# Issuing the seven products of a quarter group one by one, in an order written out for each block

## The chip, the cores and the metric

The kernel runs on one core of one Trainium2 chip, in one launch. The metric is device time in microseconds (us): the median of three runs was 294.25 us (293.95 to 294.44). Times are written to two digits after the point where they come from a trace.

## The reference

Causal attention with sparse masks, followed by a two-layer network with the Mish activation:

```python
def _attn_ref(q, k, v):                      # q, k, v: 8 x 8 x 576 x 64
    scores = scale * np.matmul(q, k.transpose(0, 1, 3, 2))
    mask_local = (rel >= 0) & (rel < stride)                  # heads 0 to 3, stride 32
    mask_strided = (rel >= 0) & (pos[None, :] % stride == pos[:, None] % stride)   # heads 4 to 7
    ...
    attn = softmax(np.where(masks, scores, -1e9))
    return np.matmul(attn, v)

def _moe_ref(x, w_in, w_out):                # x: 4608 x 512, w_in: 512 x 2048, w_out: 2048 x 512
    h = x @ w_in
    g = h * np.tanh(np.log1p(np.exp(h)))     # Mish
    return g @ w_out
```

## The kernel before

**Blocks.** The 4608 tokens are cut into nine blocks of 512, t = 0 to 8. In block t the kernel does three things side by side: the input product of block t (class `Mlp1`), the output product of block t - 1 (class `Mlp2`), and the attention of batch t + 1 (class `Attn`), as long as there is one. Attention works by batches of 576 tokens, and the MLP takes its 512 out of a ring `xT` of four batches. Blocks 0 and 1 have plans of their own, which the change leaves alone; blocks 2 to 8 are run by `run(plan, t)`. Block 2 has the plan `MAIN2`, blocks 3 to 6 `MAIN`, blocks 7 and 8 `PLAIN`, in which no attention is left.

**Seven products.** Each big product is cut into two by two blocks and computed with seven products instead of eight (Strassen's scheme in Winograd's form). It needs sums of the inputs, made by VectorE: `xs` (steps x0 to x3, the transposed tokens), `gs` (n, g1, g2, g3, the activations), and once `wis` and `wos` (the weights). x1 reads x0's result and x3 that of x1. gs1 is written twice: g1 gives what product 6 of the output reads, and g3 overwrites it for product 4. n makes gs0 for the next block, and g1 reads gs0 and the second half of the activations.

**The input product.** It goes by quarter groups g = 0 to 3 of the hidden features. A group uses three PSUM banks: E, al and be. In this order, on the left the plan's letter of before:
- `a`: product 5 into E; cast of E to s5; product 1 into al; copy of al to be by ScalarE
- `b`: product 6 added to al; cast of al to s2; product 3 added to E; VectorE adds E and s2 into one half of `hh`; product 2 added to be
- `c`: product 7 added to al; VectorE adds al and s5 into the other half of `hh`
- `d`: product 4 added to al
- `U`, `W`, `H`: ScalarE's Mish of be, of al and of `hh` into `gT`

A product is four matmuls of 256 columns. The casts run on ScalarE in blocks 1 to 6 and on VectorE in blocks 7 and 8 (`self.eng`). In blocks 2 to 6 groups 0 and 2 share one set of three banks, groups 1 and 3 the other, so that i (product 1) of group 2 has to wait for W of group 0. The set of groups 1 and 3 is also that of the output product of the block before; the set of groups 0 and 2 also serves every second score tile. In blocks 7 and 8 group 1 has the two attention banks and the E of groups 0 and 3.

**The output product.** Its seven products have two halves each of eight matmuls; a letter `m` in a plan issues the next half, in the order of products 1, 5, 2, 6, 3, 7, 4. Products 1, 5, 6 and 4 are copied by ScalarE, products 3 and 7 added by VectorE; the result goes out by SyncE's DMA queue.

**Attention.** `q0` to `q2` make the scores of the strided heads, `q3` to `q5` those of the local heads: matmuls into a pair of banks, two exps on ScalarE (tile `Ps` or `Pl`), and the mask's multiplication in place (line 287), from block 3 on by GpSimd. `v` issues the next of 13 steps: five products with V of the strided heads (v1 to v5 in the prediction; VectorE divides each by its row sum, lines 314 and 319), two transposes back, then four and two for the local heads. These steps take the banks A0 and A1 in turn. `s` spreads and shares V in its buffers (VectorE). `D` issues the DMA transposes of the next batch, `R` its loads on GpSimd's queue. `e` and `f` load ScalarE's tables for exp and for Mish.

**What sets the order.** A plan is a string of steps. Each engine gets its instructions in the order in which the steps stand, and works them off in that order; semaphores hold an instruction until its inputs are there and its buffer is free. Nothing reorders them. So a plan's order is the order of each queue.

Of the kernel before, what the change touches and what calls it, by code (L numbers as in the profile page):

```python
# [45 lines left out]
def kernel(ctx, tc, q, k, v, moe_w_in, moe_w_out, out):  # L46
    nc = tc.nc
    B, H, S, D = q.shape
# [6 lines left out]
    PE, Po, Dv, Sc = nc.tensor, nc.gpsimd, nc.vector, nc.scalar  # L55
# [6 lines left out]
    def sb(shape, name, dt=BF16):  # L62
        return const.tile(shape, dt, name=name)
# [8 lines left out]
    s2, s5 = [[sb([128, 512], f"{n}{i}", F32) for i in range(2)] for n in ("s2", "s5")]  # L72
# [36 lines left out]
    A0, A1 = bank("at0"), bank("at1")  # L109
# [6 lines left out]
    def cast(eng, out_, in_):  # L116
        if eng is Sc:
            Sc.copy(out_, in_)  # L118
        else:
            eng.tensor_copy(out_, in_)  # L120

    def add(eng, out_, a, b, op=ALU.add):
        eng.tensor_tensor(out=out_, in0=a, in1=b, op=op)  # L123
# [58 lines left out]
    def spread_v(eng):  # L182
        cast(eng, vs[0:PN, :, :, 0:D], vraw[0:PN])
# [197 lines left out]
    class Mlp1:  # L381
# [18 lines left out]
                    )  # L400

        def step(self, s, g):
            z = (self.t + g + 1) % 2
            be, al, E = [x[:] for x in SETS[z]]
            if self.eng is Dv:
                z = ((self.t + 1) % 2, 2, self.t % 2, (self.t + 1) % 2)[g]
                be, al, E = [x[:] for x in ((A1, A0, SETS[(self.t + 1) % 2][2]) if g == 1 else SETS[z])]
            h = hh[z]
            o = gT[:, 4 * g:4 * g + 4, :]
            two = lambda x: x.rearrange("p (u n) -> p u n", u=2)  # L410
            if s == "a":
                self.prod(5, g, E, True)
                cast(self.eng, s5[z][:], E)
                self.prod(1, g, al, True)
                Sc.copy(be, al)  # L415
            elif s == "b":
                self.prod(6, g, al, False)
                cast(self.eng, s2[z][:], al)
                self.prod(3, g, E, False)
                add(Dv, h[:, 0, :], E, s2[z][:])  # L420
                self.prod(2, g, be, False)
            elif s == "c":
                self.prod(7, g, al, False)
                add(Dv, h[:, 1, :], al, s5[z][:])
            elif s == "d":
                self.prod(4, g, al, False)
            elif s == "H":
                Sc.activation(  # L428
                    o[:, :, 256:512], h[:].rearrange("p i (u n) -> p (i u) n", u=2), AF.Mish
                )  # L430
            elif s == "U":
                Sc.activation(o[:, 0:2, 0:256], two(be), AF.Mish)
            elif s == "W":
                Sc.activation(o[:, 2:4, 0:256], two(al), AF.Mish)  # L434
# [130 lines left out]
    with tc.manual_schedule():  # L565
# [6 lines left out]
        B0, B1 = SETS[0][0], SETS[1][0]  # L572

        def unread(n, to, w=512):
            for _ in range(n):
                mm(to[:, 0:w], wis[:, 0, 0, 0, 0:128], wis[:, 0:2, 0, 0, 0:w // 2], True)
# [35 lines left out]
        def plain(t, fc, ps, ccs=(2, 3, 0, 1), act=True):  # L612
            r = (512 * t) % RT
            for cc in ccs:
                mm(
                    ps[:], w_in[:, cc, fc * 128:fc * 128 + 128], xT[:, cc, r:r + 512],
                    start=(cc == 2), stop=(cc == 1),
                )
            if act and ccs[-1] == 1:
                Sc.activation(gT[:, fc, :], ps[:], AF.Mish)  # L620
# [91 lines left out]
        def run(plan, t):  # L712
            b = t + 1
            m1, m2, nxt = Mlp1(t), Mlp2(t - 1), Mlp2(t)
            at = Attn(b) if b < B else None
            if b == B:
                unread(1, A1)
            ms = m2.steps() if t > 1 else []
            bank = [1, 0] if t == 1 else [0, 1]

            def v_steps():
                def pv(kind, r):
                    at.pv(kind, *r, (A0, A1)[bank[0]])
                    bank[0] = (bank[0] + bank[1]) % 2

                def xt(kind, hf):
                    at.xt(kind, hf, (A0, A1)[bank[0]], Sc if t == 1 and kind == "l" else Dv)
                    bank[0] = (bank[0] + bank[1]) % 2
                P = lambda kd, r: (lambda: pv(kd, r))
                X = lambda kd, hf: (lambda: xt(kd, hf))  # L730
                if t == 1:
                    return (
                        [P("l", r) for r in PV_L[:3]] + [X("l", 0), P("l", PV_L[3]), P("s", PV_S[0]), X("l", 1)]
                        + [P("s", r) for r in PV_S[1:]] + [X("s", 0), X("s", 1)]
                    )
                return (
                    [P("s", r) for r in PV_S] + [X("s", 0), X("s", 1)]
                    + [P("l", r) for r in PV_L[:2]] + [X("l", 0)]
                    + [P("l", r) for r in PV_L[2:]] + [X("l", 1)]
                )  # L740
            vs_ = late + (v_steps() if at else [])
            late.clear()
            JOBS = [("s", 0), ("s", 1), ("s", 2), ("l", 0), ("l", 1), ("l", 2)]
            for w in plan.split():
                c, n = w[0], int(w[1:]) if len(w) > 1 else 0
                if c in "abcdHUW":
                    m1.step(c, n)
                elif c == "p":
                    plain(t, n, deal1[n], act=False)
                elif c == "y":  # L750
                    Sc.activation(gT[:, n, :], deal1[n][:], AF.Mish)
                    if deal1[n] is A0:
                        bank[:] = [0, 1]
                elif c == "w":
                    w_out_sums(n, Dv)
                elif c == "m":
                    ms.pop(0)()
                elif c == "x":
                    x_sum(t, n, Dv)
                elif c == "g":  # L760
                    m2.g_sum(n, Dv)
                elif c == "n":
                    nxt.g_sum(0, Dv, 0, 8)
                elif not at:
                    continue
                elif c == "e":
                    Sc.preload_act_table(AF.Exp)
                elif c == "f":
                    Sc.preload_act_table(AF.Mish)
                elif c == "q":  # L770
                    at.qk(*JOBS[n], PAIRS[n % 2 * (1 + (t + 1) % 2)])
                    at.mask(*JOBS[n], Dv if t == 1 or t == 2 and n in (0, 1, 2, 3) else Po)
                elif c == "v":
                    if vs_:
                        vs_.pop(0)()
                elif c == "s":
                    spread_v(Dv)
                    if t > 1:
                        share_v(b, Dv)
                elif c == "h":  # L780
                    share_v(b, Dv)
                elif b + 1 >= B:
                    continue
                elif c == "t":
                    t_step(2, "l", "kq"[n // 2], n % 2, (C[1], C[2], A0, A1)[n], (Sc, Dv)[n % 2])
                    if n == 3:
                        load_qk(3)
                elif c == "D":
                    transpose_by_dma()
                elif c == "R":  # L790
                    hold(kTs, qTs, *((kTl, qTl) if t > 1 else ()))
                    load_vs(b + 1)
                    load_vl(b + 1)
                    if b + 2 < B:
                        load_qk(b + 2)
            assert not ms
            if t == 1:
                late.extend(vs_)
            else:
                for w in vs_:  # L800
                    w()

        late = []
        MAIN = (
            "x0 m m e m m x1 s x2 g1 g2 q0 q1 m m m m g3 q2 q3 m m q4 q5 m D v m f R a0 v v m m v v b0 a1 x3 c0 v "
            "U0 v b1 d0 U1 W0 c1 v a2 d1 W1 v H0 a3 v v b2 v H1 c2 b3 c3 d2 W2 v H3 d3 n U2 U3 W3 H2"
        )
        SECOND = (
            "t0 p0 q2 p1 t1 t2 t3 w1 p2 q3 w2 p3 q5 q4 p4 h p5 p6 f v y0 D y1 p7 s v p8 R y3 y6 v y2 v p9 v v y5 y4 "
            "p10 p11 y9 p12 y8 y7 y11 v v p13 v y13 p14 y10 p15 y14 n v y12 w3 y15"  # L810
        )
        MAIN2 = (
            "v m m v m e v x0 x1 m x2 g1 q1 q0 g2 m m m m g3 q2 s q3 m m q4 q5 m D f v m v a0 R v m m v v b0 a1 x3 "
            "c0 v v b1 d0 U0 U1 W0 c1 v a2 d1 W1 v H0 a3 v v b2 v c2 H1 b3 c3 d2 W2 v H3 d3 U2 U3 W3 H2 n"
        )
        PLAIN = (
            "m m x0 g1 x1 m m x2 x3 a0 m m g2 m b0 m m m g3 m m c0 U0 a1 H0 m m b1 d0 W0 a2 c1 a3 b2 b3 c3 d1 U2 H1 "
            "W1 U1 c2 d3 W3 U3 d2 H2 W2 H3 n"
        )

        for t in range(1, NBLK):
# [40 lines left out]
```

## Time and profile before

| | us |
|---|---|
| median of three runs | 294.25 |
| the profiled execution | 294.54 |
| its span, first to last instruction | 292.8 |
| TensorE busy (matmul ends are modelled) | 282.4 |
| VectorE, ScalarE, GpSimd busy | 205.7, 204.7, 102.7 |
| block 2, from its first half output product to the next block's | 30.31 |
| blocks 3, 4, 5, 6 | 29.60, 29.59, 29.69, 29.80 |
| blocks 7, 8 | 25.20, 25.19 |

In the profile, PE is TensorE's matmuls, PEld its weight loads, DVE VectorE, ACT ScalarE, POOL GpSimd and SP SyncE. A line of the timeline has the start in us, the length in us, the engine, the source line, the operation, the tiles written and read, shapes, and in brackets idle time of the engine before it and what ended it. Every matmul of the two products has line 129, the sums and adds line 123. Rows of one engine overlap a little, since an engine takes up the next instruction before the last one has drained: the interval from start to start tells the rate, the length tells when a result is there.

### The profile page before, as it was taken

What the parts mean: (1) busy time and instruction counts of PE and PEld (TensorE: products, weight loads), DVE (VectorE), ACT (ScalarE), POOL (GpSimd) and SP (SyncE); (2) the same over time, 40 slices, a digit from 0 to 9 for tenths busy, and PEclk for the clock granted to TensorE, in tenths of its full rate; (3) what the DMA queues carried; (4) which work ended last, traced back from release to release, by engine and by line L of the source; (5) the groups of instructions that cost most, each with busy time, mean ns of one, the idle gap of its engine ahead of it and who ended that gap; (6) DMA issues with size and microseconds to landing.
All of it is one profiled execution on the core that took longest, in us unless ns stands there. A gap on an engine that the chain in (4) does not pass through costs nothing.

```text
span 292.8 us, 7799 instructions
## 1 busy us (share of the span) xinstructions
PE 282.4 (96%) x3256; PEld 223.8 (76%) x3268; DVE 205.7 (70%) x387; ACT 204.7 (70%) x361; POOL 102.7 (35%) x109
## 2 busy tenths in 40 slices
PE   8889999999999999999999999999999999999995
PEld 3564545545788888888888888888898888888884
DVE  2583548587798896688768866886688667757842
ACT  2578793769667789778977898789878526825650
POOL 8754330131614533981399039502920000000000
PEclk9999999999999999999999999999999999999999
DMA  7999999999999999999699989950110003003004
GB/s 136 179 204 202 203 194 185 174 169 150 137 154 181 204 174 70 165 223 166 32 167 215 167 39 147 231 36 2 72 73 2 2 29 118 1 3 143 2 0 143
DMA packets 94415, 35.84 MB, mean 122 GB/s; under 512 B 75804, under 2 KB 90124, under 8 KB 94380
## 3 DMA queue, kind: packets, MB, share of 16 engines
q0 software_dynamic: 61712, 18.71, 70.1%
q1 hardware_dynamic: 31708, 15.73, 24.4%
q10 hardware_dynamic: 960, 0.91, 1.0%
q8 instruction: 25, 0.41, 0.6%
q14 instruction: 10, 0.08, 0.1%
HBM read 37.87 MB, written 9.44 MB: 162 GB/s over the span
## 4 chain that ended last, share of the span: by engine, by line
PE 77%; ACT 8%; DVE 7%; issue 3%; DMA 3%; POOL 1%; ACTq 0%; POOLq 0%
PE al L129 34%; PE ee L129 19%; PE be L129 12%; PE at L129 5%; DVE hh L123 4%; PE at L310 3%; ACT s L118 3%; DMA vraw<-in_v_dram 3%; ACT gT L428 1%; PE at L338 1%; ACT Pl L281 1%; ACT gT L434 1%; DVE x_l L319 1%; ACT be L415 1%; PE at L330 1%
## 5 line engine op out<-in xcount | busy, mean ns | idle before, releaser
L129 PEld LDWEIGHTS <-w_in 128*128 128x128 bf16 x464 | 44.3, 98 | 20.6 <-issue 5.0
L129 PEld LDWEIGHTS <-gs 128*128 128x128 bf16 x512 | 48.7, 98 | 6.3 <-DVE gs L123 0.3
L129 PEld LDWEIGHTS <-wis 128*128 128x128 bf16 x472 | 44.5, 99 | 9.2 <-issue 3.2
L129 PEld LDWEIGHTS <-gT 128*128 128x128 bf16 x448 | 42.0, 98 | 10.0
L287 POOL TENSOR_TENSOR Ps<-Ps,consts_sb 72x864 bf16<-72x864 bf16 (+1 forms) x12 | 23.2, 1957 | 48.2 <-ACT Ps L281 48.2
L123 DVE TENSOR_TENSOR gs<-gT,gs 128x2048 bf16<-128x2048 bf16 x16 | 21.0, 1312 | 15.4 <-PE al L129 9.7
L129 PE MATMUL al<-wos,gs 128*128 128x256 bf16 x256 | 31.8, 273 | 0.0
L129 PE MATMUL al<-xs,wis 128*128 128x256 bf16 x208 | 30.4, 272 | 0.1
L428 ACT ACTIVATE gT<-hh 128x1024 bf16<-128x1024 f32 x26 | 27.7, 1067 | 0.0
L129 PE MATMUL al<-xT,w_in 128*128 128x256 bf16 (+1 forms) x141 | 25.8, 300 | 1.6 <-ACT gT L434 0.9
L129 PE MATMUL be<-xT,w_in 128*128 128x256 bf16 (+1 forms) x139 | 25.1, 299 | 0.2 <-issue 0.2
L287 POOL TENSOR_TENSOR Pl<-Pl,consts_sb 128x960 bf16<-128x960 bf16 (+1 forms) x14 | 22.2, 1608 | 7.6 <-ACT Pl L281 7.6
L129 PE MATMUL be<-w_out,gT 128*128 128x256 bf16 (+1 forms) x157 | 23.3, 293 | 0.2
L314 DVE RECIPROCAL rden<-at 96x6 f32<-96x6 f32 (+2 forms) x64 | 12.1, 189 | 14.6 <-PE at L310 10.8
L434 ACT ACTIVATE gT<-al 128x512 bf16<-128x512 f32 x26 | 15.6, 601 | 7.8 <-PE al L129 7.8
L319 DVE TENSOR_TENSOR x_s<-at,rden 72x448 bf16<-72x448 f32 (+1 forms) x34 | 19.9, 585 | 1.2
L123 DVE TENSOR_TENSOR hh<-al,s 128x512 f32<-128x512 f32 x26 | 17.8, 684 | 2.8 <-PE al L129 2.4
L123 DVE TENSOR_TENSOR hh<-ee,s 128x512 f32<-128x512 f32 x26 | 17.8, 684 | 2.5 <-ACT s L118 1.9
L123 DVE TENSOR_TENSOR gs<-gT 128x2048 bf16<-128x2048 bf16 x16 | 19.5, 1218 | 0.0
L129 PE MATMUL al<-w_out,gT 128*128 128x256 bf16 (+1 forms) x143 | 19.3, 284 | 0.1
L120 DVE COPY xT<-at 128x576 bf16<-128x576 bf16 x25 | 14.5, 597 | 4.5 <-PE at L330 4.3
L319 DVE TENSOR_TENSOR x_l<-at,rden 96x384 bf16<-96x384 f32 x30 | 16.6, 553 | 1.0
(185 smaller groups left out, 573.9 us busy)
## 6 DMA issues: line engine op xcount, KB each, us to landing
out_dram<-osb SPq DMA_DIRECT2D x16, 512.0 KB, 3.4
vraw<-in_v_dram POOLq DMA_DIRECT2D x8, 288.0 KB, 6.1
w_out<-in_moe_w_out_dram POOLq DMA_DIRECT2D x4, 512.0 KB, 15.4
ql<-in_q_dram POOLq DMA_DIRECT2D x7, 288.0 KB, 10.8
vl<-in_v_dram POOLq DMA_DIRECT2D x7, 288.0 KB, 9.1
kl<-in_k_dram POOLq DMA_DIRECT2D x5, 384.0 KB, 11.0
ks<-in_k_dram POOLq DMA_DIRECT2D x6, 288.0 KB, 8.2
qs<-in_q_dram POOLq DMA_DIRECT2D x6, 288.0 KB, 9.1
```

The source lines that it names most:

```text
L118: Sc.copy(out_, in_)
L120: eng.tensor_copy(out_, in_)
L123: eng.tensor_tensor(out=out_, in0=a, in1=b, op=op)
L129: PE.matmul(o, lhsT=lhsT, rhs=rhs, start=start, stop=stop, skip_group_check=True)
L281: Sc.activation(pt[0:n, e, 0:o], ps[e][0:n, 0:o], AF.Exp, scale=scale)
L287: meng.tensor_tensor(out=pm, in0=pm, in1=mk[0:n, :].unsqueeze(1).unsqueeze(1).to_broadcast([n, 2, nu, w]), op=ALU.mult,)
L310: PE.matmul(po[:, n - n0, :], lhsT=pt[0:r, c0:c0 + 128], rhs=rhs, start=True, stop=True)
L314: Dv.reciprocal(rden[0:m, 0:nu], po[0:m, :, D])
L319: Dv.tensor_tensor(out=x[0:m, n0:n1, :], in0=po[0:m, :, 0:D], in1=rden[0:m, 0:nu].unsqueeze(2).to_broadcast([m, nu, D]), op=ALU.mult,)
L330: PE.transpose(tr[:, WQ * w:WQ * w + WQ], x_l[0:WQ, u:u + 2, :].rearrange("p u d -> p (u d)"), ident[0:WQ, 0:WQ],)
L428: Sc.activation(o[:, :, 256:512], h[:].rearrange("p i (u n) -> p (i u) n", u=2), AF.Mish)
L434: Sc.activation(o[:, 2:4, 0:256], two(al), AF.Mish)
```

## The change

`Mlp1.step` no longer issues a, b as units. Product 1 with its copy becomes a step `i`, product 3 with its add `j`, product 2 `k`; `a` is now product 5 and its cast, `b` product 6 and its cast. A capital `A` or `B` puts the cast on the other engine. All three plans are written anew: the steps are the same in number, but their order is another for each group. Among what moves are also steps that are not part of the input product: in `MAIN` g1 is now the first step of the block, with s, x0, x1, g2 and x2 behind it, and q0, q1 stand one half output product earlier.

```diff
         def step(self, s, g):
+            eng = self.eng
+            if s in "AB":
+                s, eng = s.lower(), Dv if eng is Sc else Sc
...
             if s == "a":
                 self.prod(5, g, E, True)
-                cast(self.eng, s5[z][:], E)
+                cast(eng, s5[z][:], E)
+            elif s == "i":
                 self.prod(1, g, al, True)
                 Sc.copy(be, al)
             elif s == "b":
                 self.prod(6, g, al, False)
-                cast(self.eng, s2[z][:], al)
+                cast(eng, s2[z][:], al)
+            elif s == "j":
                 self.prod(3, g, E, False)
                 add(Dv, h[:, 0, :], E, s2[z][:])
+            elif s == "k":
                 self.prod(2, g, be, False)
...
-                if c in "abcdHUW":
+                if c in "ABabcdijkHUW":
                     m1.step(c, n)
...
         MAIN = (
-            "x0 m m e m m x1 s x2 g1 g2 q0 q1 m m m m g3 q2 q3 m m q4 q5 m D v m f R a0 v v m m v v b0 a1 x3 c0 v "
-            "U0 v b1 d0 U1 W0 c1 v a2 d1 W1 v H0 a3 v v b2 v H1 c2 b3 c3 d2 W2 v H3 d3 n U2 U3 W3 H2"
+            "g1 s m m m x0 x1 g2 e q0 q1 m x2 m m m m q2 q3 g3 m m q4 q5 m v D m R a0 f v i0 v m v m v b0 A1 i1 v k0 "
+            "j0 c0 x3 b1 j1 v k1 d0 U0 c1 W0 U1 a2 i2 v d1 v W1 A3 H0 i3 v b2 j2 b3 v H1 c2 k2 v c3 k3 d2 j3 n W2 U2 "
+            "v H2 d3 W3 U3 H3"
         )
...
         MAIN2 = (
-            "v m m v m e v x0 x1 m x2 g1 q1 q0 g2 m m m m g3 q2 s q3 m m q4 q5 m D f v m v a0 R v m m v v b0 a1 x3 "
-            "c0 v v b1 d0 U0 U1 W0 c1 v a2 d1 W1 v H0 a3 v v b2 v c2 H1 b3 c3 d2 W2 v H3 d3 U2 U3 W3 H2 n"
+            "e m v m v m v g1 x0 x1 m x2 q1 q0 g2 m m m m g3 q2 q3 m s m q4 q5 m D v m R v a0 i0 m f v v B0 m v j0 k0 "
+            "x3 a1 i1 c0 v v b1 k1 d0 c1 U0 U1 W0 j1 a2 v i2 d1 W1 H0 a3 v b2 i3 v v j2 k2 v c2 H1 b3 U2 j3 k3 U3 c3 "
+            "d2 W2 v H3 d3 W3 H2 n"
         )
         PLAIN = (
-            "m m x0 g1 x1 m m x2 x3 a0 m m g2 m b0 m m m g3 m m c0 U0 a1 H0 m m b1 d0 W0 a2 c1 a3 b2 b3 c3 d1 U2 H1 "
-            "W1 U1 c2 d3 W3 U3 d2 H2 W2 H3 n"
+            "x0 x1 x2 g1 x3 m g2 m m a0 m m i0 m m B0 m m k0 j0 g3 m m m A1 c0 i1 m U0 b1 d0 m W0 j1 H0 a2 i2 c1 a3 "
+            "k1 i3 b2 j2 U1 B3 j3 k3 c3 k2 c2 d1 H1 d3 U2 W1 W3 d2 n U3 W2 H2 H3"
         )
```

## The prediction

> **What bounds the kernel now.** I read the page first, then the stretches, then the timeline of one block.
>
> ```profile
> PE 282.4 (96%) x3256; PEld 223.8 (76%) x3268; DVE 205.7 (70%) x387; ACT 204.7 (70%) x361; POOL 102.7 (35%) x109
> ...
> PEclk9999999999999999999999999999999999999999
> ...
> PE 77%; ACT 8%; DVE 7%; issue 3%; DMA 3%; POOL 1%; ACTq 0%; POOLq 0%
> ```
>
> TensorE is never throttled and carries the chain. Matmul ends are modelled, so I measure it by starts: the four matmuls of one product take 0.437 us from the start of one product to the next when nothing waits (129.45 to 129.89 below), a half of the output product ("m") 0.873. Next the blocks, cut at the first m of each: t = 2, then 3 to 6, then 7 and 8.
>
> ```profile
> 77.45:107.76 30.31, 29.94 (x386) 26.05 (x383) 26.86 (x54) 21.81 (x41) 11.08 (x14) 1.00 1.89 176
> 137.36:166.95 29.59, 29.23 (x366) 25.61 (x364) 22.57 (x43) 24.41 (x44) 17.47 (x16) 1.00 1.27 146
> 251.64:276.83 25.19, 24.87 (x227) 21.88 (x225) 17.85 (x27) 12.94 (x22) 0.00 (x0) 1.00 0.12 43
> ```
>
> (Columns: length, busy PE, PEld, DVE, ACT, POOL, clock, DMA.) A change of order can only win what TensorE loses between starts. In the timeline of block t = 3 I looked for starts that are late:
>
> ```profile
> 129.45 0.60 PE L129 MATMUL al<-xT,w_in 128*128 128x256 bf16 x4
> 129.89 0.60 PE L129 MATMUL al<-xs,w_in 128*128 128x256 bf16 x4
> ...
> 130.51 0.60 PE L129 MATMUL ee<-xs,wis 128*128 128x256 bf16 x4
> ...
> 130.65 0.59 ACT L434 ACTIVATE gT<-al 128x512 bf16<-128x512 f32 x1
> ...
> 131.30 0.60 PE L129 MATMUL al<-xT,w_in 128*128 128x256 bf16 x4 [0.19 <-ACT gT L434]
> ...
> 136.19 0.68 DVE L123 TENSOR_TENSOR hh<-al,s 128x512 f32<-128x512 f32 x1
> ...
> 136.92 0.60 PE L129 MATMUL al<-xs,w_in 128*128 128x256 bf16 x4 [0.17 <-DVE hh L123]
> ```
>
> 130.51 to 131.30 is 0.79, so 0.35 over: a3's product 1 starts bank al afresh and must wait until W1 has read it. The product at 136.34 to 136.92 is 0.34 over: d3 waits for c3's add. With 0.07 at 133.72 (an s2 cast) that is **0.75 us a block**, 0.93 in t = 2 and 0.74 in t = 7 and 8 (275.52 to 276.38 holds 0.43 of it, waiting for c2's add). All that can be won in seven blocks is 0.93 + 4 x 0.75 + 2 x 0.74 = 5.4 us.
>
> **Return trips**, from these rows: a product ends its issue 0.20 before the engine can start on it (d1 ends issue at 130.33; DVE and ACT rows that wait start 0.20 behind), an ACT read of 512 columns ends 0.59 later, the next product starts 0.06 after: 0.85. By DVE 0.20 + 0.69 + 0.04 = 0.93. Back to back, ACT rows start 0.49 apart, DVE adds 0.60.
>
> **What the change removes in the blocks' second half.** Work per engine is the same but for casts: two a block leave ACT for DVE in t = 3 to 6, one in t = 2; three go the other way in t = 7 and 8. They cost nothing by themselves, since both engines idle over 15% of a block; what counts is which read comes late.
> - MAIN: between d1 and i3 still lie only one PV (0.18) and A3 (0.437), 0.62 where 0.85 is needed; but A3's cast has left ACT, so W1 starts 0.03 late instead of 0.12. i3 loses 0.26 instead of 0.35. c2 has k2 and a PV more in front of it: the 0.07 goes. c3's add now has k3, d2, j3 and the transposes before d3 (1.57 us against 0.93), and only DVE's queue (the PV of v12, then the add) holds it: 0.03. So 0.29 for 0.75: **0.46 x 4 = 1.85**.
> - MAIN2: b2 now lies between W1 and i3, so that wait goes; g1 first on DVE ends the 0.18 at 82.95; c3 and d3 lose 0.04 + 0.23. 0.27 for 0.93: **0.65**.
> - PLAIN: b3, c3 and c2 get other products in front; at the end d3 is followed by d2 alone (0.437) before the next m, which needs W3's read of that bank (0.85): 0.42, and d2 0.06. 0.48 for 0.74: **0.26 x 2 = 0.5**.
> Sum 3.0 us won if nothing new is late. Bounds: nothing, and 5.4.
>
> **What it adds at the blocks' start.** In MAIN the plan began with x0 and put g1 behind x0, x1, the spread and x2. Now g1 is first on DVE. g1 reads the last Mish (H3), so the spread copy, the share, x0, x1, g2 and x2 queue behind that wait; DVE idles about 1.4 us and does them all after H3. Order on ACT is H3, the copy of product 1, the table load, q0's two exps; then POOL masks q0. Take H3's end as 0. ACT by its rows (139.41, 140.35, 140.99, then 1.29 to the next, exps 0.42 apart and 0.53 long): q0's second exp ends at 2.76, POOL starts 0.15 later, **2.91**. DVE by its rows (0.03 behind H3; 1.14 for g1, 0.71 spread, 0.50 share, 0.45 x0): x1 starts at **2.83**, g2 at 3.18, x2 at 4.32; g3 waits for the last reader of gs1 (m 6), about 4.75. So four DVE sums with both inputs in SBUF stand against three POOL masks. Before, only g3 did, and this is what it cost:
>
> ```profile
> 143.86 1.81 POOL L287 TENSOR_TENSOR Ps<-Ps,consts_sb 72x864 bf16<-72x864 bf16 x1 [11.37 <-ACT Ps L281]
> ...
> 145.15 1.60 DVE L123 TENSOR_TENSOR gs<-gT,gs 128x2048 bf16<-128x2048 bf16 x1 [2.14 <-PE al L129]
> ...
> 145.64 2.79 POOL L287 TENSOR_TENSOR Ps<-Ps,consts_sb 72x864 bf16<-72x864 bf16 x1
> ```
>
> g3 comes at 145.15, ends 1.08 after the first mask's end (145.67) and is 0.38 longer than the 1.22 of g1 and g2; the second, equal mask is 0.98 longer and ends 1.68 after g3. They run one after the other, and the one that waited goes next, ahead of the other engine's next instruction. The adds that read a PSUM bank do not do this (masks over them keep their length). The Trainium skill, "SBUF — State Buffer", section "Who interferes with whom", says that a DVE instruction with two SBUF inputs and a GpSimd one that reads SBUF exclude each other for the whole instruction and that issue order decides who blocks; the rows agree, with 0.38 and 0.98.
>
> **The forecast's sum: they take turns.** Put 0 at the block's first m (H3 ends at 3.04; 3.12 before). x1 5.87 to 6.29; mask q0 to 8.05; g2 (1.08 behind it) 9.13; mask q1 (1.68) 10.81; x2 11.1; mask q2 (1.15) 12.25; g3 13.33. DVE works in order: behind g3 wait the output add of product 3 and v1's reciprocal and multiplication (0.60 + 0.22 + 0.62), done 14.69. TensorE reaches v3, which needs v1's bank, at 13.43 and starts at 14.73: 1.30. v4 needs v2's bank, read by 16.08 behind product 7's add, and loses 0.27. Together **1.57 us in each of t = 3 to 6, 6.3 us**. The blocks' second half then finds DVE caught up (A1's cast is its next deadline). Net: 6.3 - 3.0 = 3.3 us slower. The profiled execution took 294.54 (span 292.8 and 1.7 around it), so 297.8 by it; it is 0.29 over the median of 294.25, so by the median **297.6**.
>
> Hidden: the wait for H3 itself, since m 6 reads gs1 from 5.84 on and g1 is done at 4.3; POOL's later end, since the L masks (4.9 us more) end by 18.5 and L's first PV is at 22; the loads behind them move by under a microsecond against a block of 29. If that cover went, the next block's spread would wait for its 288 KB (6.1 us median to land). SP's and POOL's queues keep their instructions and their order.
>
> **Rivals.**
> - **DVE keeps its turn.** g2 and x2 follow x1 without a gap, and a gapless follower may go before a waiting mask; no row shows a mask waiting for two DVE sums. Then x2 ends at 7.77, the masks (1.68 or 1.8, 1.8, 1.2 and once g3) end at 13.4 to 13.6, and v2, whose sixth matmul at 12.93 needs mask q2, waits 0.6. 4 x 0.6 - 3.0 = -0.6: **293.7**.
> - **The masks have room** (not slower). Alone they need 4.9 us from 5.94, 10.8, against 12.93: 2.1 us of cover. If x1 and g2 are through before q0's exps are, 0.6 us earlier or the exps 1.6 later than my chains say, only g3 collides as before, and what is won stays: 294.25 - 3.0 = **291.3**. For it: all deadlines in the second half then hold by my table. Against it: both chains hang on the same H3, so a shift of the block moves neither.
> - **The mask is first.** x1 is ahead of it by 0.08 us only. Turned round, L0's mask too comes ahead of g3, g2 is late for m 7 (0.5) and v1's bank free at 16.7: 3.5 a block, **305**.
> - That the order isn't what the diff says is excluded: the built program's queues show g1 first, two casts on DVE, and the same instructions otherwise.
>
> **Numbers.** Turns 0.42, DVE keeps 0.26, room 0.26, mask first 0.06. Under 0.2% (0.6 us) this kernel can't be told from no change. Faster: all of room and half of DVE keeps, 0.39; the same: a third of DVE keeps and a little of turns, 0.11; slower 0.50. The range takes in turns with two full waits (2.0 a block, 299.3) and goes down to the case of room, 291.3 to 299.6; turns alone would have 296 to 299.6.
>
> **What would show it.** Right: in t = 3 to 6, x1, g2 or x2 of 1.5 us and more instead of 0.42 and 1.22, masks of 1.8 to 2.9, and a PV that starts 1.3 late some 13.5 us into the block; blocks of 30.7, 29.7 for t = 2, 24.9 for t = 7 and 8. Wrong: masks and sums at their lone lengths and blocks near 29.1 (room); long masks but short sums and a late second PV (DVE keeps). The steps of the second half show by themselves: product 1 of group 3 late by 0.26, d3 hardly.

## The result, and the profile after

The changed kernel took 321.47 us (median of four runs, 320.23 to 325.4) against 294.35 of the kernel before beside it (293.95 to 294.50): the ratio is **1.091, interval 1.085 to 1.097**. The 325.4 counts as a slow run, so it is left out of the ratio. The profiled execution took 320.25 us, with a span of 318.5. The prediction of 297.6 (291.3 to 299.6) had the sign of its forecast right and the size wrong by 24 us.

The page of the changed kernel, in the rows that were shown of the kernel before:

```profile
PE 290.0 (91%) x3256; PEld 227.8 (72%) x3268; DVE 239.7 (75%) x390; ACT 203.3 (64%) x358; POOL 106.6 (33%) x109
...
PEclk9999999999999999899979997899959999999999
```

TensorE has as many matmuls as before, but 7.6 us more busy time, and its clock, which was never throttled, now has four dips. VectorE is 34.0 us busier with three instructions more. The stretches of the blocks (t = 2, then 3 to 6, then 7; columns as before: length, busy PE, PEld, DVE, ACT, POOL, clock, DMA):

```profile
77.33:107.65 30.32, 29.91 (x391) 26.18 (x388) 27.46 (x55) 22.40 (x42) 11.55 (x14) 1.00 1.82 174
107.65:143.66 36.01, 30.89 (x366) 26.46 (x364) 31.60 (x43) 22.48 (x40) 18.21 (x16) 0.95 1.43 144
143.66:177.87 34.21, 30.83 (x366) 26.38 (x364) 29.67 (x45) 23.36 (x42) 18.60 (x16) 0.95 0.96 124
177.87:215.12 37.25, 31.29 (x367) 26.68 (x365) 32.43 (x45) 23.37 (x42) 14.49 (x12) 0.91 0.54 84
215.12:252.71 37.59, 31.64 (x367) 26.91 (x365) 32.63 (x46) 23.60 (x43) 11.00 (x6) 0.91 0.08 29
252.71:277.63 24.92, 24.69 (x226) 21.91 (x224) 16.83 (x25) 14.63 (x25) 0.00 (x0) 1.00 0.12 44
```

All of the loss is in blocks 3 to 6: 145.06 us against 118.68 before, 26.4 more. Blocks 7 and 8 won 0.28 each, block 2 nothing. Inside block t = 5, VectorE's timeline:

```profile
183.72 0.43 DVE L123 TENSOR_TENSOR xs<-xT,xs 128x512 bf16<-128x512 bf16 x1
184.07 2.84 DVE L123 TENSOR_TENSOR gs<-gT 128x2048 bf16<-128x2048 bf16 x1
186.83 7.19 DVE L123 TENSOR_TENSOR xs<-xT 128x512 bf16<-128x512 bf16 x1
193.94 1.93 DVE L123 TENSOR_TENSOR gs<-gT,gs 128x2048 bf16<-128x2048 bf16 x1
195.79 0.68 DVE L123 TENSOR_TENSOR osb<-ee,o 128x512 f32<-128x512 f32 x1
196.39 0.19 DVE L314 RECIPROCAL rden<-at 72x7 f32<-72x7 f32 x1
196.61 0.62 DVE L319 TENSOR_TENSOR x_s<-at,rden 72x448 bf16<-72x448 f32 x1
```

The rows from the top are x1, g2, x2, g3, the add of product 3, and v1's two. x2 is the sum that takes 0.43 us alone: it took **7.19**. GpSimd's timeline beside it (a row with x2 holds the mask that starts there and the one behind it):

```profile
183.77 2.06 POOL L287 TENSOR_TENSOR Ps<-Ps,consts_sb 72x864 bf16<-72x864 bf16 x1 [15.54 <-ACT Ps L281]
185.79 4.02 POOL L287 TENSOR_TENSOR Ps<-Ps,consts_sb 72x864 bf16<-72x864 bf16 x2
188.55 1.27 POOL L287 TENSOR_TENSOR Ps<-Ps,consts_sb 72x576 bf16<-72x576 bf16 x1
189.78 2.00 POOL L287 TENSOR_TENSOR Pl<-Pl,consts_sb 128x960 bf16<-128x960 bf16 x1
191.75 3.04 POOL L287 TENSOR_TENSOR Pl<-Pl,consts_sb 128x960 bf16<-128x960 bf16 x2
```

x2 stands from 186.83. L0 to L2 are the masks of q3 to q5. The masks of q1 (to 188.58), q2 (to 189.81), L0 (to 191.78) and L1 (to 193.73) all go by, and x2 ends 0.29 behind the last of these. In blocks 3 to 6, x2 took 5.40, 3.35, 7.19 and 7.20, each time until a mask's end. Everything behind it on VectorE is late, v1's multiplication too, and TensorE waits for that (waits of PE: us in all, times, longest; then its timeline):

```profile
PE at L310 <- DVE x_s L319: 19.4, 4, 5.8
```

```profile
190.88 0.60 PE L129 MATMUL al<-xT,w_in 128*128 128x256 bf16 x4
197.29 0.55 PE L310 MATMUL at<-vs,Ps 72*128 72x65 bf16 x7 [5.80 <-DVE x_s L319]
197.88 1.86 PE L129 MATMUL al<-w_out,gs 128*128 128x256 bf16 x8
199.54 0.59 PE L310 MATMUL at<-vs,Ps 72*128 72x65 bf16 x7
199.94 1.80 PE L129 MATMUL al<-w_out,gs 128*128 128x256 bf16 x8
```

v3 starts at 197.29 instead of 191.32 (190.88 + 0.437). And what follows is slow: the half at 197.88 takes 1.66 to the next start where 0.873 is usual, 0.213 us a matmul instead of 0.109. The stretch of that time has the clock in the third column from the end:

```profile
194.70:201.50 6.80, 4.16 (x30) 3.08 (x30) 5.39 (x11) 0.00 (x0) 3.55 (x7) 0.50 0.58 97
```

TensorE was idle from 191.3, its granted clock fell to 0.50 from 194.7 and came back at 201.5. By starts, and against the same blocks of the run in which only the sums' place was put back (the first experiment), the loss is, in us (from unrounded starts, so a length can differ by 0.01 from the stretches above):

| block | v3 late | half behind v3, waits for the add of product 7 | slow matmuls after it | sum | block minus its length there |
|---|---|---|---|---|---|
| 3 | 4.96 | 0.39 | 1.53 | 6.88 | 36.02 - 29.15 = 6.87 |
| 4 | 3.22 | 0.39 | 1.46 | 5.07 | 34.21 - 29.15 = 5.06 |
| 5 | 5.97 | 0.39 | 1.75 | 8.11 | 37.24 - 29.15 = 8.09 |
| 6 | 5.96 | 0.39 | 1.90 | 8.25 | 37.60 - 29.37 = 8.23 |

So 20.1 us are the wait itself, 1.6 the add and 6.6 the clock, and nothing over 0.02 us a block is left over.

### The profile page after: what moved, and what is told of

Read it like the earlier page. It is cut to its first block, busy times and chain, and to the rows that moved or that the text cites. A ratio compares the mean times of both kernels' runs of the same rounds, so it can differ in the third digit from the quotient of the medians.

```text
span 318.5 us, 7803 instructions
## 1 busy us (share of the span) xinstructions
PE 290.0 (91%) x3256; PEld 227.8 (72%) x3268; DVE 239.7 (75%) x390; ACT 203.3 (64%) x358; POOL 106.6 (33%) x109
## 4 chain that ended last, share of the span: by engine, by line
PE 77%; DVE 9%; ACT 6%; issue 6%; DVEq 0%; ACTq 0%
PE al L129 33%; PE ee L129 18%; PE be L129 14%; PE at L129 4%; DVE gs L123 3%; PE at L310 3%; DVE osb L123 2%; DVE xs L123 2%; ACT gT L440 2%; ACT Pl L281 1%; PE at L330 1%; PE at L338 1%; ACT be L419 1%; ACT gT L438 1%; DVE x_s L319 1%
## 5 line engine op out<-in xcount | busy, mean ns | idle before, releaser
L129 PEld LDWEIGHTS <-gs 128*128 128x128 bf16 x512 | 51.3, 103 | 9.8 <-issue 1.4
L129 PEld LDWEIGHTS <-w_in 128*128 128x128 bf16 x464 | 43.0, 98 | 17.6 <-issue 2.4
L310 PE MATMUL at<-vs,Ps 72*128 72x65 bf16 x220 | 13.4, 204 | 19.4 <-DVE x_s L319 19.4
L123 DVE TENSOR_TENSOR gs<-gT,gs 128x2048 bf16<-128x2048 bf16 x16 | 23.5, 1466 | 9.7 <-ACT gT L434 8.6
L310 PEld LDWEIGHTS <-Ps 72*128 72x128 bf16 x256 | 13.8, 104 | 23.0 <-issue 20.1
L123 DVE TENSOR_TENSOR xs<-xT 128x512 bf16<-128x512 bf16 x14 | 27.3, 1953 | 0.1
L123 DVE TENSOR_TENSOR gs<-gT 128x2048 bf16<-128x2048 bf16 x16 | 26.0, 1623 | 0.7 <-ACT gT L440 0.7
L287 POOL TENSOR_TENSOR Pl<-Pl,consts_sb 128x960 bf16<-128x960 bf16 (+1 forms) x14 | 24.0, 1734 | 7.5 <-ACT Pl L281 7.5
L533 ACT COPY osb<-al 128x512 f32<-128x512 f32 x7 | 4.1, 585 | 30.2 <-PE al L129 30.2
L129 PE MATMUL al<-w_out,gs 128*128 128x256 bf16 x128 | 22.4, 336 | 0.8 <-DVE osb L123 0.7
```

The source lines that it names most:

```text
L129: PE.matmul(o, lhsT=lhsT, rhs=rhs, start=start, stop=stop, skip_group_check=True)
L287: meng.tensor_tensor(out=pm, in0=pm, in1=mk[0:n, :].unsqueeze(1).unsqueeze(1).to_broadcast([n, 2, nu, w]), op=ALU.mult,)
L310: PE.matmul(po[:, n - n0, :], lhsT=pt[0:r, c0:c0 + 128], rhs=rhs, start=True, stop=True)
L533: Sc.copy(osb[:, :, 256:512], halves(al))
```

## The experiments

The theory: the place of the sums in MAIN (g1 first) brings x2 beside the masks, where it waits out one mask after another; all else of the change is a small gain. The rivals: the new order of products and casts costs time by itself; the size or the place of x2 is what makes it lose; the clock adds nothing of its own. In the diffs the plans are cut to the steps that differ.

**1. The sums of before, all else of the change.**

```diff
-            "g1 s m m m x0 x1 g2 e q0 q1 m x2 m m m m q2 q3 g3 ...
+            "x0 m m m x1 s x2 g1 g2 e q0 q1 m m m m m q2 q3 g3 ...
```

> The changed kernel, but in blocks 3 to 6 VectorE's steps x0, x1, s, x2, g1, g2 stand ahead of the masks again, in the order of before; TensorE's and ScalarE's orders stay those of the change. Theory (VectorE's sums with two SBUF inputs and GpSimd's masks exclude each other, and a sum that loses its turn holds up VectorE's queue): x2 takes 0.42 us again, only g3 meets a mask, blocks 3 to 6 take 29.1 to 29.3 us, and the whole 291 to 292.5 us. Rival (the products issued one by one make the PV steps late, whatever the sums do): blocks stay at 34 us and more, the whole over 310.

Measured: 291.83 us against 294.56, ratio 0.9914, interval 0.9891 to 0.9937. Stretches of blocks 3 and 7:

```profile
107.60:136.75 29.15, 29.05 (x366) 25.50 (x364) 24.08 (x43) 22.35 (x40) 17.79 (x16) 1.00 1.43 168
...
224.43:249.34 24.91, 24.68 (x225) 21.89 (x224) 16.84 (x25) 14.62 (x25) 0.00 (x0) 1.00 0.12 44
```

In block 4 VectorE is done with x2 (140.36) before the first mask starts at 142.65. g2 (141.83) still runs for 0.4 us then and keeps its 1.22; the mask takes 2.08 instead of 1.81. Of the sums only g3 waits for a mask:

```profile
140.36 0.43 DVE L123 TENSOR_TENSOR xs<-xT 128x512 bf16<-128x512 bf16 x1
...
141.83 1.22 DVE L123 TENSOR_TENSOR gs<-gT 128x2048 bf16<-128x2048 bf16 x1
144.54 1.27 DVE L123 TENSOR_TENSOR gs<-gT,gs 128x2048 bf16<-128x2048 bf16 x1 [1.49 <-PE al L129]
```

The loss is the sums' place, and the rest of the change wins 0.44 a block (29.59 to 29.15).

**2. The other way round: the kernel before with the sums in their new place** (q0, q1 and the table load move with them, g3 goes behind q2 and q3, and D behind the first step with V).

```diff
-            "x0 m m e m m x1 s x2 g1 g2 q0 q1 m m m m g3 q2 q3 m m q4 q5 m D v m f R ...
+            "g1 s m m m x0 x1 g2 e q0 q1 m x2 m m m m q2 q3 g3 m m q4 q5 m v D m f R ...
```

> The kernel before, with nothing of the change but the first half of block 3 to 6: g1 first, then s, x0, x1, g2 and x2, and q0, q1 half an output product earlier; the products stay in their old units and all casts on ScalarE. Theory: x2 waits for two to five masks, v3 or v2 starts 3 to 6 us late, blocks 3 to 6 take 34 to 38 us, the whole 315 to 325. Rival (the loss needs the new order of the products): within 2 us of 294.

Measured: 320.04 us. Blocks 3 to 6 took 38.65, 34.89, 34.72 and 34.64 (29.60, 29.59, 29.69, 29.80 before), x2 5.41, 3.27, 3.27, 3.27; block 3 lies 0.65 above the expected 38. Its x2:

```profile
119.78 5.41 DVE L123 TENSOR_TENSOR xs<-xT 128x512 bf16<-128x512 bf16 x1
```

The move alone brings the loss, without a new product or cast.

**3. The sums in their new place, the masks on VectorE.**

```diff
-                    at.mask(*JOBS[n], Dv if t == 1 or t == 2 and n in (0, 1, 2, 3) else Po)
+                    at.mask(*JOBS[n], Po if t == 2 and n > 3 else Dv)
```

> The changed kernel with the masks of blocks 3 to 6 on VectorE instead of GpSimd. Theory: there is nobody to take turns with, every sum has its lone length (0.42 and 1.22), and although VectorE has 3.3 us a block more to do, blocks take 29.2 to 30.2, the whole 291.5 to 295.5. Rival (VectorE's queue is late by its own work, GpSimd is only a witness): with more work on VectorE the blocks get longer still than 36.

Measured: 295.85 us, blocks 30.05, 30.05, 30.05, 30.27, no sum longer than alone. A mask is much shorter here, two of them in 1.12:

```profile
145.26 1.12 DVE L287 TENSOR_TENSOR Ps<-Ps,consts_sb 72x864 bf16<-72x864 bf16 x2
```

Without GpSimd in the masks the waits are gone, so the loss needs both engines; 0.9 a block stays (v3 0.52 and the half behind it 0.39 late), since VectorE has the masks to do itself. The time is 0.35 above what was expected.

**4. x2 ahead of g2**, so that the short sum comes earlier and the long g2 takes its place.

```diff
-            "g1 s m m m x0 x1 g2 e q0 q1 m x2 m m m m ...
+            "g1 s m m m x0 x1 x2 g2 e q0 q1 m m m m m ...
```

> The changed kernel with x2 in front of g2 in blocks 3 to 6. In the changed kernel the long sums g2 and g3 got the port at the first end of a mask that they met, 8 times of 8, x2 lost 9 of 13 ends. If the place in the run of masks decides (the first end goes to VectorE, later ones mostly to GpSimd), x2 now waits for one mask and g2 for several: g2 of 4 to 8 us, product 7 of the output late, the whole 315 to 330. If the sum's size decides, x2 loses several ends and g2 behind it one: x2 of 4 to 7 us, g2 of 2.9. If it is chance, neither pattern holds in all four blocks.

Measured: 322.71 us. x2 now waits out one mask (2.04), g2 one (2.84; 1.21 without a wait in block 3), and g3 loses in its turn, 6.2 us in each block:

```profile
151.13 2.84 DVE L123 TENSOR_TENSOR gs<-gT 128x2048 bf16<-128x2048 bf16 x1
153.89 6.21 DVE L123 TENSOR_TENSOR gs<-gT,gs 128x2048 bf16<-128x2048 bf16 x1
```

None of the three patterns came: g2, the second sum to wait in blocks 4 to 6, won the first end that it met, and the third lost. So it is not x2 itself that loses, and a long sum loses as well.

**5. TensorE kept busy:** twenty matmuls that nobody reads ahead of group 0's product 1, in blocks 3 to 6.

```diff
             elif s == "i":
+                if g == 0 and 2 < self.t < 7:
+                    unread(20, be)
                 self.prod(1, g, al, True)
```

> The changed kernel with 20 matmuls of 512 columns, whose result nobody reads, in front of group 0's product 1 in blocks 3 to 6 (4.3 us of TensorE's time a block, in the stretch that it would spend waiting for v3's bank). It adds work and takes none away. Theory (the sums' wait is VectorE's and GpSimd's alone, and a part of the loss is the half clock that the traces show behind TensorE's wait): VectorE's times do not move, the wait before v3 shrinks by about 4 us, the rows behind it run at 0.109 us a matmul instead of 0.213, the granted clock is 1.0, and blocks 3 to 6 are 1.0 to 1.5 us shorter than the changed kernel's where its wait was 5 us or more; the whole 315 to 319. Rival (the clock costs nothing, the rows behind it have slack): the block keeps its length or grows by what the filler is too long, 321 to 326.

Measured: 312.61 us, with 4.3 us of work *added* to each block; the clock over the whole run was 0.999. x2 took 5.41, 3.35, 3.35 and 7.19, so its wait in block 5 was another than in the changed kernel, and that block can't be compared. The three with an equal wait: 34.51 instead of 36.02, 33.47 instead of 34.21, 35.71 instead of 37.60. In blocks 3 and 6 that is 1.51 and 1.89 less, the table's 1.53 and 1.90. The half behind v3 runs at the usual rate, here in block 3 (0.87 to the next start):

```profile
126.32 0.37 PE L310 MATMUL at<-vs,Ps 72*128 72x65 bf16 x7 [0.49 <-DVE x_s L319]
126.92 1.03 PE L129 MATMUL al<-w_out,gs 128*128 128x256 bf16 x8 [0.23 <-DVE osb L123]
127.79 0.38 PE L310 MATMUL at<-vs,Ps 72*128 72x65 bf16 x7
```

So the slow clock is a cost of its own, and idle time causes it. In block 4 only 0.74 of 1.46 came back: the added 4.3 us outlast that block's wait of 3.2.

**6. The remaining waits mended**, on top of 1: in MAIN b2 before i3 and k2 before b3, in PLAIN other products ahead of the last m, in MAIN2 a PV ahead of the half that waits for an output add.

```diff
-  ... v W1 A3 H0 i3 v b2 j2 b3 v H1 c2 k2 v c3 ...          (MAIN)
+  ... v W1 A3 b2 i3 H0 v j2 k2 b3 v H1 c2 v c3 ...
-  ... k2 c2 d1 H1 d3 U2 W1 W3 d2 n U3 ...                    (PLAIN)
+  ... k2 c2 H1 d3 U2 W3 d1 W1 d2 n U3 ...
-  ... R v a0 i0 m f v v B0 ...                               (MAIN2)
+  ... R v a0 i0 v m f v B0 ...
```

> The sums ahead of the masks as in the first run, and the three waits that were left in its trace taken away by order alone: in block 3 to 6 b2 between W1 and product 1 of group 3; in blocks 7 and 8 d3 ahead of d1 and d2, with W3 behind it; in block 2 one PV step ahead of the output's product 4. By the return trips (0.85 by ScalarE, 0.93 by VectorE): blocks 3 to 6 from 29.15 to 28.9 (28.85 to 29.0), blocks 7 and 8 from 24.91 to 24.5, block 2 from 30.3 to 30.1; the whole 2.0 us below the first run, 289 to 290.5. Rival (the waits only move to the next read): within 0.5 us of the first run.

Measured: 293.25 us, ratio 0.9955 (0.9938 to 0.9972), a miss. PLAIN's blocks (24.52) and block 2 (30.09) came as expected, but the output's last part is 0.3 longer, and MAIN got worse, 29.66: the wait at i3 is gone and a longer one stands ahead of d2 (product 4 of group 2), which needs c2's add on VectorE,

```profile
134.53 0.60 PE L129 MATMUL be<-xT,w_in 128*128 128x256 bf16 x4
135.56 0.60 PE L129 MATMUL al<-xs,w_in 128*128 128x256 bf16 x4 [0.43 <-DVE hh L123]
```

1.03 from start to start where a product takes 0.44. The rival of this run was right in MAIN: the wait moved to the next read.

**7. A gap behind each mask:** a GpSimd instruction that needs no sum's input.

```diff
                     at.mask(*JOBS[n], Dv if t == 1 or t == 2 and n in (0, 1, 2, 3) else Po)
+                    if t > 2:
+                        y = small.tile([32, 1], BF16, tag="hold", name="hold")
+                        Po.memset(y[:], 0.0)
```

> The changed kernel with a small write by GpSimd (32 x 1, reads nothing) behind each mask of blocks 3 to 6. If VectorE loses a mask's end only because the next mask follows without a gap, it now gets its turn at each end: x2 waits for one mask (about 1.8 us), blocks take 30.5 to 31.5, the whole 297 to 300, as the prediction had it. If what decides lies elsewhere, x2 still loses ends: x2 of 3 to 7 us in most blocks, the whole 312 to 325.

Measured: 320.13 us; x2 took 5.47, 5.47, 5.47 and 3.32, so a write in between does not give the sum its turn. The gap that it made was next to none, though: the write takes 0.09, and a mask now starts up to 0.01 behind the end of its predecessor instead of 0.03 ahead of it. What a longer gap would do is not shown.

**8. Masks of half the size**, each as two instructions.

```diff
+            if meng is Po and self.b > 3:
+                for e in range(2):
+                    add(
+                        meng, pm[:, e], pm[:, e],
+                        mk[0:n, :].unsqueeze(1).to_broadcast([n, nu, w]), ALU.mult,
+                    )
+                return
```

> The changed kernel with each mask of blocks 3 to 6 as two instructions of half the size. If a waiting sum gets in at one end of a mask in two or so, by chance, the waits halve: x2 of 1 to 4 us, the whole 303 to 314. If GpSimd runs its queue through once it has beaten a sum, x2 still waits until the last masks: 315 to 326. If exclusion were not by whole instruction, x2 would take its share of each mask and no end would show in its length.

Measured: 321.39 us, blocks 36.77, 35.43, 36.96 and 36.91. The first waits shrink (g2 2.0 instead of 2.84), but the sum that loses is passed by more of the smaller masks: g3 took 7.6 in block 3 and 5.6 in block 6, x2 5.7 and 6.7 in blocks 4 and 5. So the wait is not one instruction of the other engine, it lasts until the burst is nearly over.

**9. Another try at the remaining waits:** 6 with MAIN as in 1, but a PV ahead of i3.

```diff
-  ... v W1 A3 H0 i3 v b2 j2 ...
+  ... v W1 A3 H0 v i3 b2 j2 ...
```

> The sums first in MAIN, as in the run of that name (291.83), with three waits of its second half and of the other plans taken out: a PV goes ahead of product 1 of group 3 (0.18 of its 0.26), PLAIN's last product 4 has two products behind it before the bank is needed (0.4 in block 7; in block 8 as much goes to the output's last part), and MAIN2 loses the 0.39 for an output add. My theory: blocks 30.1, 28.95 to 29.0 four times, 24.5, 24.5, and 290.2 to 291.0 in all. If the change's second half instead does not bear its own order without the masks' disturbance, a new wait of 0.3 or more shows behind the PV that moved, and the time stays at 291.8 or above.

Measured: 292.85 us, ratio 0.9946 (0.9933 to 0.9959). The rival of this run was right: blocks of 29.55, since the PV that came forward now has the transposes too close behind it. They start 0.54 late, in the middle of their row of six, waiting for VectorE's division of that PV.

**10. The changed kernel once more**, as it is.

> The changed kernel itself, nothing edited. If which engine goes next at a mask's end is settled by chance, x2 waits 2 to 7.2 us in another pattern over blocks 3 to 6 than 5.40, 3.35, 7.19, 7.20, and the four blocks add up to another sum than 145.1 (between 137 and 150 by the blocks seen so far: 34.2 to 37.6 each). If the program fixes it, the four waits come again within 0.1.

Measured: 316.53 us. x2 took 5.40, 3.35, **3.35** and 7.19, and block 5 34.15 instead of 37.24. In that block, in the same program at the same place:

```profile
183.60 2.84 DVE L123 TENSOR_TENSOR gs<-gT 128x2048 bf16<-128x2048 bf16 x1
186.36 3.35 DVE L123 TENSOR_TENSOR xs<-xT 128x512 bf16<-128x512 bf16 x1
189.64 3.02 DVE L123 TENSOR_TENSOR gs<-gT,gs 128x2048 bf16<-128x2048 bf16 x1
```

```profile
188.08 1.27 POOL L287 TENSOR_TENSOR Ps<-Ps,consts_sb 72x576 bf16<-72x576 bf16 x1
189.31 2.26 POOL L287 TENSOR_TENSOR Pl<-Pl,consts_sb 128x960 bf16<-128x960 bf16 x1
```

The sum goes at the end of q2's mask (189.35), and the next mask waits (2.26 instead of 2.00). So that end is not settled by the program: three blocks came again, one did not.

**11. x2 behind the masks**, the rest as in the change.

```diff
-            "g1 s m m m x0 x1 g2 e q0 q1 m x2 m m m m ... f v i0 v m v m v b0 ...
+            "g1 s m m m x0 x1 g2 e q0 q1 m m m m m ... f v i0 v m v m v x2 b0 ...
```

> The changed kernel with x2 alone moved behind the fifth step with V, when the masks are over. If only the first end of a burst of masks goes to VectorE, g2 still waits out one mask and g3, which is now the second sum that waits, loses as x2 did: 3 to 7 us, v3 late by 2 to 5, blocks of 31 to 36. If x2 is what loses (the short one), g3 waits out one mask as in the kernel before, 1 to 2 us, v3 is late by under 0.7, and the blocks are 29.2 to 30.

Measured: 315.69 us. g3, which now comes behind g2, loses as x2 did: 6.21, 7.98, 4.16 and 8.00 (up to 1.0 above what was expected), blocks 36.01, 37.27, 30.62 and 36.01. In block 4:

```profile
153.19 7.98 DVE L123 TENSOR_TENSOR gs<-gT,gs 128x2048 bf16<-128x2048 bf16 x1
```

So what loses is the sum that stands there in the middle of the burst, whichever it is.

**12. What won, put together:** MAIN as in 1, PLAIN and MAIN2 as in 6.

> MAIN exactly as in the run with the sums first (29.15 a block), and of the mending only what showed its gain twice: PLAIN's order at the end (24.52 a block, the output's last part 0.32 longer) and MAIN2's exchange (30.1). By those blocks: 291.83 - 0.19 - 2 x 0.39 + 0.32 = 291.2, and 290.9 to 291.5. If the blocks are not independent of one another, MAIN is not 29.15 here and the time is 291.8 or more.

Measured: 291.49 us (median of ten), ratio 0.9902, interval 0.9873 to 0.9930. Blocks 30.10, then 29.16 three times and 29.37, 24.52 twice, as expected; the median is at the upper edge of what was expected, beside a kernel before that was at 294.75 here. (The profiled execution, 294.17, starts its blocks 2.8 us later than that of run 1; the blocks are equal.) By the interval it is 0.7 to 1.3% shorter than the kernel before, a small gain; from run 1 it can't be told apart, the two intervals overlap.

## Why the prediction was wrong

**Right.** That the four sums and the masks meet, where and in which order: x1 ahead of q0's mask by 0.04 to 0.06 in blocks 4 to 6 (0.08 predicted), g2 and x2 among the masks. That they exclude each other for whole instructions. That v1's division hangs behind g3 and v3 waits for it, with nothing else late in between. That the wait for H3 costs nothing.

**The failed step** is "They run one after the other, and the one that waited goes next, ahead of the other engine's next instruction". That was read from one kind of event, the first mask's end with g3 waiting, of which the kernel before had four. It holds there and not later. Over the kernel before, the changed kernel and runs 2, 4, 5, 7, 10 and 11, I counted the ends at which a sum waited and a mask was queued behind:

| a mask's end | VectorE's sum goes | the next mask goes |
|---|---|---|
| first of a burst (q0) | 32 | 0 |
| q1 | 6 | 16 |
| q2 | 10 | 18 |
| L0 | 9 | 18 |
| L1 (one small mask left) | 18 | 0 |

Between the first and the last, the sum that waited lost 52 times of 77. So the terms were: x2 was to wait out one mask and end 2.0 behind g2 (9.13 to 11.1), and took 3.35 to 7.20; **v3 was to be 1.30 late, measured 3.22 to 5.97**, 20.1 us in four blocks instead of 5.2. The 0.27 at v4 for v2's bank did not come; 0.39 was lost at the half that follows v3, which waits for the add of product 7 itself.

The Trainium skill, "SBUF — State Buffer", section "Who interferes with whom", which the prediction weighed here, has two parts. The exclusion for the whole instruction agrees with every row above. That issue order decides who blocks does not agree with this trace: x2 stood from 186.83, and three masks that started at 188.55, 189.78 and 191.75 went ahead of it. Their inputs came behind it too: the last exp of each ended at 186.85, 187.76 and 189.37. The measurement decides.

**The missing step.** Nothing in the prediction asked what TensorE does after an idle time of microseconds, since before it never had one: "TensorE is never throttled" was a fact of that order and not of the kernel. That is 6.6 of the 28.3 us. The Trainium skill, "TensorE: Matmul & The Clock Gate", Part 1, has the clock halved after an idle window of about 3.4 us and the windows on a grid that runs by itself; the slow pieces agree, 3.41 us twice and 6.83 twice, at 0.5. An idle window in full was not needed: in block 4 TensorE was idle for 3.2 us, and the clock fell, at 160.57; the 3.41 us before that hold 0.23 us of matmuls.

**The sums that won.** MAIN's second half was worth 0.46 a block by my count and 0.44 in run 1; i3's 0.26 came as 0.265, and d3 lost nothing. PLAIN's 0.26 came as 0.28. MAIN2's 0.65 came as nothing: the wait at b2 and its like went, but a half of product 4 now starts 0.39 late behind product 7's add, for which VectorE must first divide a PV (91.00 to 91.82 from start to start, where a product takes 0.44), and d3 loses 0.35 instead of 0.23. Run 6 cut the first of these from 0.39 to 0.17, and the block fell to 30.09.

**The rivals.** None of them came. "DVE keeps its turn" failed at its first step: g2 followed x1 without a gap and still waited out a mask (2.84 instead of 1.22). "The masks have room" is what runs 1 and 12 reach by another order (291.8 and 291.5, where it said 291.3). "The mask is first" came true in block 3 alone: x1 started 0.02 behind the mask and took 2.07, but the block was not the longest. Forecast and rivals shared the step that failed: no row before showed what a *second* waiting sum does, and for this unseen event the range had none, one mask and at most two full waits as bounds. The far bound, a sum that waits until the burst is over, was left out; with v3 late by the 6.0 then measured in four blocks it is 294.25 + 24 - 3 = 315 without the clock, and far outside the range given.

**Open.** Which rule settles a mask's end. The size of the sum, the size of the mask, a small write in between and x2 itself do not settle it (runs 4, 8, 7 and 11); a real gap between the masks was not tried. That ScalarE is at work at that moment is excluded too: sums won and lost with it busy and idle. How long the next mask has had its inputs separates the ends of q1's mask: the sum went all six times that q2's exps had ended 0.6 to 0.9 us before, the mask all sixteen times that they had ended 1.7 to 1.9 before. But at q2's end the mask went with L0's exps done 1.05 before, and at q0's end the sum with q1's done 1.06 to 1.38 before, so no one limit fits them all. The end of q2's mask is a tie: in thirteen passes of blocks 4 to 6 (the changed kernel, runs 5, 7, 10 and 11) ScalarE's last exp ended within 0.03 us of it; the sum went in all seven in which the exp ended before the mask or with it, and the mask in all six in which it ended 0.003 to 0.016 after. But in run 2 the sum went though an exp ended 0.15 after, and in its block 3 the mask though the exp ended 0.004 before; in run 4 the mask went though the exp was done 0.16 to 0.19 before. So this is no rule yet. It fits that executions of one program differ, 320.2 to 322.7 us and 316.5 in run 10.

## What to carry to other kernels

Before you move a VectorE instruction with both inputs in SBUF, look which GpSimd instructions will be running then: beside a burst of them, take as the far bound that it waits until the burst is nearly over, and count everything behind it in VectorE's order. A rule read from one kind of event holds for that kind; if the change makes a second event follow the first, take the bound from the longest chain that can form. And where TensorE would be idle for as long as here, 3.2 us and more, add what it loses afterwards at half clock.

## What the runs showed of the hardware

- A VectorE sum of 0.43 us took up to 7.20 us beside a burst of six GpSimd masks; one was running when it came, and three that started later went ahead of it. With masks of half the size, g3 of 1.22 us took 7.6.
- In eight runs the first end of a burst went to the waiting sum 32 times of 32, the last one with a mask still behind it 18 of 18, and those between 25 of 77.
- After 3.2 to 6 us without work, TensorE ran at half clock in pieces of 3.41 or 6.83 us: 0.213 us instead of 0.109 a matmul of 256 columns, 1.46 to 1.90 us lost in a block. Unread matmuls in the idle time kept the clock and made the blocks 1.5 and 1.9 us shorter.
- A mask of 72x864 takes 1.8 us on GpSimd and 0.56 on VectorE (two in 1.12, run 3).
